# Moving a weight slice to another queue, new planned landing times, and 90 instead of 95 pairs of exponentials on VectorE

## The chip, the cores and the metric

The kernel runs on one core of a Trainium2 chip. The metric is the device time of one execution in microseconds (us). Four runs of the kernel before took 880.51 to 882.28 us, with a median of 881.9. The engines are named as the profile names them: PE (TensorE, with PEld for its weight loads), DVE (VectorE), ACT (ScalarE), POOL (GpSimd) and SP (SyncE, which only issues transfers here). SPq and ACTq in a row are transfers being issued by these engines.

## The reference

Two branches work on the same x (2048 tokens, 640 wide) and are mixed by a gate. Branch A is a short causal convolution of k over four steps, a product with v, a convolution along all 2048 tokens by FFT, and a product with x. Branch B is attention with 32 heads of 20 columns that share one k and one v.

```python
def _B_ref(x, wq, wk, wv, wo):
    q = (x @ wq).reshape(B, S, 32, 20).transpose(0, 2, 1, 3)
    k, v = x @ wk, x @ wv                       # one head of 20 columns
    p = softmax(einsum("bhqd,bkd->bhqk", q, k) * 20 ** -0.5)
    o = einsum("bhqk,bkd->bhqd", p, v)
    return o.transpose(0, 2, 1, 3).reshape(B, S, 640) @ wo

x = A_q
g = sigmoid((x * gate_w).sum(-1, keepdims=True))
a = _A_ref(x, A_k, A_v, A_shift_k, A_ssm_k, A_ssm_D)
b = _B_ref(x, B_wq, B_wk, B_wv, B_wo)
return g * a + (1 - g) * b
```

All inputs and the output are bf16.

## The kernel before

**A planner writes the order.** The kernel first builds a graph of operations (`Op`: an engine, a function that emits the instruction, what it depends on, a price in us, a priority). `Scheduler.run` then plays the five engines against each other with these prices and puts each operation into its engine's list. Only the order of these lists, and the semaphore waits that follow from the dependences, go into the program: prices and latencies in the code are never executed. On the chip each engine works through its list strictly in order, and an instruction that waits holds up all that stand behind it. The planner's numbers are `LAT` (L17, 0.12 us from the end of one operation to the start of one on another engine that depends on it), `SLACK` (L18), the price functions `c_ps`, `c_fast`, `c_exp`, `c_act`, `c_pool`, `c_mm` (L595 to L616), and, for transfers, `nbytes / 300e3` plus `lat` (L432 to L438).

**The attention stream.** Scores are computed in tiles of 128 keys by 512 queries for one head: 4 query blocks x 8 groups of four heads x 16 key blocks x 4 heads = 2048 tiles. `stream` (L1096) walks over 32 groups G and 16 key blocks j. ACT takes the exponential of most tiles, in units that are alternately three tiles wide (written to ETA) and two tiles wide (ETB), one ACTIVATE for each unit (L1161). Their scores come from `QK` (L1136, matmuls at L1129) into PSUM banks 0 to 2 and 3 to 4, and their products with v go through `PV` (L1202) into bank 6. The next unit's scores can be written only when ACT has read the same banks two units earlier. For the j named in `DVE_J[G]` (L590), two of the four tiles, "a pair", go to DVE: `DEXP` (L1165) computes a polynomial exponential in five instructions (two L1191, then L1194, L1195, L1197). Its score matmuls ride along with those of a unit, and its products with v are added before the group's last product. L590 names 95 pairs.

**Side work.** PE, DVE and POOL fit the rest into the stream: the query projections of later blocks (`qproj`, L1047 and L1058), the convolution over four steps (L1385), the FFT as matmuls with cosine and sine tables (`spectra` L1442, `mac` L1475 on POOL, `inverse` L1508) and the output projection (L1538, L1301). On PE such a matmul may be planned ahead of the next score matmuls if its price is not above the planned gap plus `SLACK` (L362, L372). If nothing fits, filler matmuls (L1590) are planned.

**Before the stream.** `loads` (L788) issues four blocks of x on SP, and on ACT's queue the key weights wkr, the value weights wvr, the first slice of the query weights (100 KB, 80 of 640 columns, into `wqst`) and the gate weights gwr. SP issues the rest of the query weights after the last x block has landed. PE transposes x (L960); DVE and ACT copy the transposes to `xT` (L675, L676). While PE has nothing, `pick_work` (L386) plans filler matmuls (L1595). `weights` copies wkr and wvr (L933) and gwr (L935) into one tile on DVE, and the slice of the query weights into `wq_pad` on POOL (L938). Then come the first query group (L1047, L1058), a bound on its length (L1062, L1070, L1076, and a small transfer of the row `cr` into qT), keys, values and gate for each x block in one group of matmuls ("kvn", L987), the squared length of the keys (L995, L1006), its maximum (L1009 to L1023), and the keys with that bound in an added row (L979, L1033, L1031). Beside this run the sine tables: arguments on DVE (L859, L862), the function on ACT (L864). The first exponential needs the first query group with its row, and the first 128 keys, which wait for the maximum over all four blocks.

**After the stream** the last group is normalised and projected (`tail`, L1308).

Of the kernel before, what the change touches and what calls it, by code (L numbers as in the profile page):

```python
# [15 lines left out]
NLANES = 40  # L16
LAT = 0.12  # L17
SLACK = 0.3  # L18
FILL = 0.7
# [18 lines left out]
class Op:  # L38
    __slots__ = ("eng", "fn", "deps", "cost", "kind", "name", "prio", "grp", "alts", "port", "nbytes", "main",
                 "cont", "nun", "succ", "ready", "start", "end", "placed", "sig", "value", "lane", "known", "seq",  # L40
                 "banks", "last", "urge", "floating", "tail", "attached", "lat", "iss", "row", "soft", "cols", "hole")

    def __init__(self, eng, fn, cost, kind, name, prio):
        self.eng = eng
        self.fn = fn
# [112 lines left out]
class Scheduler:  # L158


    def __init__(self, graph, bank_free=(0, 1, 2, 3, 4, 5, 6, 7)):
        self.g = graph
        self.order = {e: [] for e in ENGS}
        self.linear = []
        self.t = {e: 0.0 for e in ENGS}
        self.bank_ready = {b: 0.0 for b in range(8)}
# [103 lines left out]
    def pool_may(self, t):  # L270
# [7 lines left out]
        return bool(w) and t > min(w)  # L278

    def pick_pe(self, t):  # L280
        op = self.pick_work(t)
# [15 lines left out]
        return made[0]  # L297

    def pick_work(self, t):
        q = self.main_q["pe"]  # L300
        p = self.main_pos["pe"]
        m = q[p] if p < len(q) else None
        gap = 1e9
        self.gap = 0.0
        if self.float_left:
# [32 lines left out]
        if m is not None:  # L338
# [5 lines left out]
            if m.nun == 0:  # L344
                r = m.ready
                ok = True
                for b in m.banks or ():
                    if not self.bank_claimed[b]:
                        if self.bank_busy[b]:
                            ok = False  # L350
                        r = max(r, self.bank_ready[b])
                if ok:
                    if r <= t:
                        self.main_pos["pe"] += 1
                        return m
                    gap = r - t
        sw = SWITCH if self.mode != "f" else 0.0
        self.gap = gap if m is not None else 0.0
        if self.open is not None:
            gr = self.open  # L360
            mm = gr.mms[gr.pos]
            if mm.ready <= t and mm.cost + sw <= gap + SLACK and (sw == 0.0 or gap + SLACK - sw >= ROOM):  # L362
                return mm
            return None
        if self.mode != "f" and self.main_started and gap + SLACK - sw < ROOM:
            return None
        best = None
        held = any(gr.rides and gr.ready <= t for gr in self.gcand)
        for gr in self.gcand:
            if gr.rides and t - gr.ready < PATIENCE:  # L370
                continue
            if gr.ready <= t and gr.mms[0].cost + sw <= gap + SLACK:  # L372
                b = None
# [38 lines left out]
    def place(self, op, e):  # L412
# [64 lines left out]
        if gr is not None:  # L477
# [4 lines left out]
            elif op in gr.evacs:  # L482
                if all(x.placed for x in gr.evacs):
                    b = gr.bank
                    self.bank_busy[b] = False
                    self.bank_last[b] = [gr.mms[-1]] + list(gr.evacs)
                    self.bank_ready[b] = max(x.end for x in gr.evacs) + LAT
        for s in op.succ:
            s.nun -= 1
            lat = 0.0 if (s.eng == "pe" and e == "pe") else LAT  # L490
            s.ready = max(s.ready, op.end + lat)
# [103 lines left out]
def c_ps(n):  # L595
    return 0.16 + 1.04e-3 * n
# [6 lines left out]
def c_exp(n):  # L603
    return 0.0633 + 0.8333e-3 * n

# [5 lines left out]
def c_pool(n):  # L611
    return 0.21 + 1.78e-3 * n

# [5 lines left out]
class Kernel:  # L619
# [419 lines left out]
    def qproj(self, I, gs, prio, banks, ng):  # L1039
# [4 lines left out]
        for gl, gi in enumerate(gs):  # L1044
            gr = self.group("qp", prio, banks=banks)
            for dc in range(NDC):
# [4 lines left out]
                if dc == 0:  # L1051

                    o.deps.update(self.crow0 or ())
                    if self.crow0:
# [62 lines left out]
    def attention(self):  # L1117
# [18 lines left out]
        def QK(n):  # L1136
# [10 lines left out]
            for k, (G, j, r) in enumerate(un):  # L1147
# [502 lines left out]
```

## Time and profile before

| | |
|---|---|
| median of four runs | 881.9 us |
| the profiled execution | 881.93 us, of which the span of the profile is 880.1 |
| busy on PE / ACT / DVE / POOL | 856.4 / 855.5 / 717.1 / 377.0 us |
| first exponential starts | 25.27 us |
| last exponential ends | 870.44 us |
| exponentials on ACT | 372 of three tiles, 371 of two |
| pairs on DVE | 95 |

A row of a timeline gives start, length, engine, line, operation, the tile written and the tiles read, and in brackets the idle time before it and what ended that. A row of groups gives the same for all instructions of a line: how often, busy time in all, mean length, idle time before them.

Busy time of each engine in five stretches (columns: stretch, its length, then busy us and number of instructions for PE, PEld, DVE, ACT and POOL, then the clock granted to PE, the transfers' share and GB/s):

```profile
0.00:25.27 25.27, 18.76 (x196) 11.68 (x199) 14.23 (x51) 12.96 (x22) 7.89 (x28) 0.93 0.52 145
140.00:675.00 535.00, 528.44 (x4815) 213.22 (x4811) 458.24 (x550) 532.87 (x471) 264.37 (x223) 1.00 0.08 23
675.00:790.00 115.00, 113.43 (x1120) 45.02 (x1117) 99.25 (x106) 115.00 (x103) 64.04 (x51) 1.00 0.04 12
790.00:870.44 80.44, 79.88 (x683) 34.61 (x679) 44.70 (x65) 80.44 (x71) 3.81 (x3) 1.00 0.25 71
870.44:880.10 9.66, 4.76 (x38) 2.78 (x36) 6.19 (x10) 0.00 (x0) 0.00 (x0) 0.88 0.20 69
```

### The profile page before, as it was taken

The numbers are of one execution on the slowest core, as the hardware profiler recorded it, in microseconds if no ns is written. First come the engines' busy times: TensorE is split into PE (matmuls) and PEld (weight loads), VectorE is DVE, ScalarE is ACT, GpSimd is POOL, SyncE is SP. The second block draws the span as 40 slices with busy tenths as digits, with TensorE's granted clock in tenths as the row PEclk, the third lists the DMA queues.
The fourth block names the chain that finished last, engine by engine and source line by source line (L and its number), as shares of the span: only waits on it lengthen the run. The fifth ranks groups of instructions, "written<-read, shape, count | busy, mean of one in ns | idle before, by whom it ended". The sixth has DMA issues, their size and how long they took to land.

```text
span 880.1 us, 18454 instructions
## 1 busy us (share of the span) xinstructions
PE 856.4 (97%) x7939; PEld 351.3 (40%) x7956; DVE 717.1 (81%) x909; ACT 855.5 (97%) x765; POOL 377.0 (43%) x351
## 2 busy tenths in 40 slices
PE   7999999999999999999999999999999999999997
PEld 4334433334334433344433323444343444324433
DVE  5668998998999888986889898778778888888444
ACT  4999999999999999999999999999999999999995
POOL 2663001445665154564352652344747335760000
PEclk9999999999999999999999999999999999999999
DMA  5910020000100000020000011100010000004221
GB/s 160 216 39 8 20 43 21 19 6 17 43 21 20 15 18 10 19 44 20 13 12 16 21 43 40 31 16 12 19 44 20 14 14 11 5 28 96 66 73 38
DMA packets 49712, 30.69 MB, mean 35 GB/s; under 512 B 32477, under 2 KB 45662, under 8 KB 49630
## 3 DMA queue, kind: packets, MB, share of 16 engines
q1 hardware_dynamic: 48254, 29.03, 12.2%
q8 instruction: 62, 1.02, 0.5%
q10 hardware_dynamic: 1376, 0.48, 0.3%
q14 instruction: 20, 0.16, 0.1%
HBM read 17.85 MB, written 6.02 MB: 27 GB/s over the span
## 4 chain that ended last, share of the span: by engine, by line
ACT 66%; PE 30%; DVE 3%; DMA 1%; issue 0%; ACTq 0%; DVEq 0%
ACT ETA L1161 39%; ACT ETB L1161 26%; PE ps L1129 9%; PE ps L1442 7%; PE ps L1202 5%; PE ps L1508 3%; PE ps L1538 2%; PE ps L1590 1%; DMA gwr<-in_gate_w_dram 1%; PE ps L1301 1%; DVE ETd L1197 1%; DVE dX L1195 1%; PE ps L979 0%; DVE dW L1191 0%; PE ps L1446 0%; DVE dX L1194 0%
## 5 line engine op out<-in xcount | busy, mean ns | idle before, releaser
L1161 ACT ACTIVATE ETA<-ps 128x1536 bf16<-128x1536 f32 x372 | 572.9, 1540 | 3.0 <-PE ps L1129 2.4
L1161 ACT ACTIVATE ETB<-ps 128x1024 bf16<-128x1024 f32 x371 | 415.0, 1119 | 0.5 <-PE ps L1129 0.5
L1129 PE MATMUL ps<-qT,kT 32*128 32x512 bf16 x2048 | 297.8, 384 | 9.6 <-ACT ETA L1161 4.5
L1475 POOL TENSOR_TENSOR Pp<-X,K 128x512 f32<-128x512 bf16 x120 | 158.8, 1340 | 154.3 <-DVE ETd L1197 36.4
L1191 DVE TENSOR_SCALAR dW<-ps 128x512 f32<-128x512 f32 x190 | 130.5, 687 | 63.6 <-PE ps L1129 62.3
L1129 PEld LDWEIGHTS ps<-qT,kT 32*128 32x128 bf16 x2048 | 73.4, 91 | 233.9 <-ACT ETB L1161 110.9
L1202 PE MATMUL ps<-ETA,vaug 128*32 128x512 bf16 x1116 | 153.1, 385 | 0.0
L1202 PE MATMUL ps<-ETB,vaug 128*32 128x512 bf16 x742 | 147.3, 385 | 0.0
L1197 DVE SCALAR_TENSOR_TENSOR ETd<-dX,dW 128x1024 int16<-128x1024 f32 x95 | 134.0, 1411 | 5.5 <-PE ps L1202 5.1
L1195 DVE SCALAR_TENSOR_TENSOR dX<-dX,dW 128x1024 f32<-128x1024 f32 x95 | 136.4, 1436 | 0.3
L1194 DVE SCALAR_TENSOR_TENSOR dX<-dW 128x1024 f32<-128x1024 uint16 x95 | 134.3, 1413 | 0.9
L1475 POOL TENSOR_TENSOR AB<-Pp 128x256 bf16<-128x256 f32 x80 | 65.0, 812 | 88.8 <-DVE dX L1194 32.8
L1442 PE MATMUL ps<-ssm_kT,Tcs 128*128 128x256 bf16 x600 | 95.5, 275 | 0.4 <-DVE dW L1191 0.4
L1442 PE MATMUL ps<-kv,Tcs 128*128 128x256 bf16 x600 | 89.2, 275 | 0.0
L1508 PE MATMUL ps<-AB,Tcs 128*128 128x256 bf16 x600 | 88.8, 274 | 0.0
L1590 PE MATMUL ps<-Tcs,zeros 128*32 128x512 bf16 x980 | 81.0, 385 | 1.1 <-DVE acc L1264 0.6
L1475 POOL TENSOR_TENSOR Pp<-Pp 128x512 f32<-128x512 f32 x40 | 57.3, 1432 | 52.7 <-DVE dX L1194 16.1
L1276 POOL TENSOR_TENSOR oTn<-acc,rbc 128x512 bf16<-128x512 f32 x24 | 41.2, 1717 | 71.1 <-DMA rbc<-scr_d 28.8
L1442 PEld LDWEIGHTS ps<-ssm_kT,Tcs 128*128 128x128 bf16 x600 | 48.3, 97 | 44.3 <-issue 31.4
L1442 PEld LDWEIGHTS ps<-kv,Tcs 128*128 128x128 bf16 x600 | 49.5, 98 | 37.5 <-issue 30.2
L1508 PEld LDWEIGHTS ps<-AB,Tcs 128*128 128x128 bf16 x600 | 51.3, 98 | 31.8 <-issue 26.7
L1202 PEld LDWEIGHTS ps<-ETA,vaug 128*32 128x32 bf16 x1116 | 29.9, 94 | 36.1 <-issue 34.5
(131 smaller groups left out, 634.5 us busy)
## 6 DMA issues: line engine op xcount, KB each, us to landing
rbc<-scr_d SPq DMA_DIRECT2D x31, 256.0 KB
scr_o<-oTn SPq DMA_DIRECT2D x24, 128.0 KB, 1.7
xn<-in_A_q_dram SPq DMA_DIRECT2D x4, 640.0 KB
kv<-in_A_v_dram SPq DMA_DIRECT2D x4, 640.0 KB, 5.0
out_dram<-outsb SPq DMA_DIRECT2D x14, 160.0 KB, 2.4
oTp<-scr_o SPq DMA_DIRECT2D x12, 160.0 KB, 2.5
wog<-in_B_wo_dram SPq DMA_DIRECT2D x4, 200.0 KB
wo<-in_B_wo_dram SPq DMA_DIRECT2D x4, 200.0 KB
```

The lines of the kernel that those rows point to most:

```text
L1129: return e.matmul(self.bank(bk), T["kT4"][32 * r:32 * r + 32, 128 * j:128 * j + 128], T[f"qT{G // 8 % 2}"][32 * r:32 * r + 32, G % 8, :], ...
L1161: op("act", lambda e: e.activation(et(n)[:, 0:w], self.ps[:, lo:lo + w], ACT.Exp, scale=SCALE), [("ps", base[n % 2] + k) for k in range(le ...
L1191: self.evac(gr, "dve", lambda e, bk, h=h: e.tensor_scalar(W[:, 512 * h:512 * h + 512], self.bank(bk), SCALE * LOG2E * 128.0, 128.0 * (127 ...
L1194: V(lambda e: e.scalar_tensor_tensor(X[:, :], w, DP, w, ALU.add, ALU.mult), [kW], ["dX"], c_ps(1024), **k)
L1195: V(lambda e: e.scalar_tensor_tensor(X[:, :], X[:, :], DQ, w, ALU.add, ALU.mult), [kW], ["dX"], c_ps(1024), **k)
L1197: V(lambda e: e.scalar_tensor_tensor(T[f"ETd{pe}"][:, :].bitcast(dt.int16), X[:, :], DA, W[:, :], ALU.mult, ALU.add), [kW, "dX"], [("ETd", ...
L1202: return op("pe", lambda e: e.matmul(self.bank(6)[32 * r:32 * r + 32, :], T[va][:, j, :], src, start=(j == 0), stop=(j == NSC - 1), tile_p ...
L1276: self.pool(lambda e: e.tensor_tensor(out, T["acc"][:, :], T["rbc"][:, :], ALU.mult), ["acc", "rbc"], [key], c_pool(512), prio=p, port=Tru ...
L1442: self.mm(gr, lambda e, bk, lhs=lhs, rhs=rhs, comp=comp, n=n: e.matmul(self.bank(bk, 256, 256 * comp), lhs, rhs, start=(n == 0), stop=(n = ...
L1475: f = lambda e: e.tensor_tensor(out, a, b, alu)
L1508: self.mm(gr, lambda e, bk, lhs=lhs, fc=fc, comp=comp, h=h: e.matmul(self.bank(bk, 256, 256 * h), lhs, AB[:, fc, :, comp, :], start=(fc == ...
L1590: sch.filler = [[lambda e, r=r, st=st: e.matmul(self.bank(6)[32 * r:32 * r + 32, :], self.T["zeros"][:, 0:32], self.T["Tcos"][:, 0, 0:512] ...
```

## The change

Three things change.

First, the load of the slice `wqst[:, :, 0:80]` moves from ACT's queue to SP's, where it stands between x block 0 and x block 1. The gate weights follow directly on the value weights on ACT's queue.

Second, the planner's numbers for the time before the stream: an engine's clock starts at 0.75 instead of 0, the latency from one engine to another comes from a table `LATS` (0 to 0.27) and is 0.03 after a transfer, and each load has a new size and latency. In the stream the latency is `LATX` (0.12) for all, and the slack is 0.3 as before, now under the names SLA, SLB and SLACK0. The price of POOL's operations and of DVE's copy of a query group change a little. `room` is defined and not called.

Third, `DVE_J` is another list, with 90 pairs: 0 0 2 1 3 4 3 3 in the first eight groups (before 0 2 3 2 4 4 2 3), then 4 5 0 4 4 1 3 3 (3 4 4 2 3 1 5 2), 3 4 4 2 2 3 2 4 (4 4 4 1 4 4 1 5) and 4 1 5 2 4 3 3 4 (5 3 1 5 5 2 1 2).

```diff
-LAT = 0.12
-SLACK = 0.3
+LAT = 0.1
+LATS = {("pe", "act"): 0.27, ("act", "pe"): 0.265, ("pe", "dve"): 0.2, ("act", "dve"): 0.265, ("act", "pool"): 0.265,
+        ("dve", "pe"): 0.06, ("dve", "act"): 0.06, ("dve", "dve"): 0.0, ("dve", "pool"): 0.08, ("act", "act"): 0.1,
+        ("pool", "pool"): 0.0}
+BEGIN = 0.75
+LATX = 0.12
+CEX = 0.0633
+LATM = {}
+SLA = 0.3
+SLB = 0.3
+SLACK = 0.05
+SLACK0 = 0.3
...
-        self.t = {e: 0.0 for e in ENGS}
+        self.t = {e: BEGIN for e in ENGS}
...
+    def bank_wait(self, m):
+        return any(self.bank_busy[b] and not self.bank_claimed[b] for b in m.banks or ())
...
+    def lat_of(self, op, a, b):
+        if self.main_started:
+            return LATM.get((a, b), LATX)
+        return 0.03 if op.kind == "d" else LATS.get((a, b), LAT)
+
+    def room(self, m, r):
+
+        q, p = self.main_q["act"], self.main_pos["act"]
+        u = m.unit
+        if p > u:
+            return 0.0
+        return max(self.t["act"] + sum(q[i].cost for i in range(p, u)) - 0.216 - LATS["pe", "act"] - r, 0.0)
...
+                if m.unit is not None and not self.bank_wait(m):
+                    slack = SLB if m.unit % 2 else SLA
+        if slack is None:
+            slack = SLACK0
...
-            if mm.ready <= t and mm.cost + sw <= gap + SLACK and (sw == 0.0 or gap + SLACK - sw >= ROOM):
+            if mm.ready <= t and mm.cost + sw <= gap + slack and (sw == 0.0 or gap + slack - sw >= ROOM):
...
-                    self.bank_ready[b] = max(x.end for x in gr.evacs) + LAT
+                    self.bank_ready[b] = max(x.end + (LATX if self.main_started else LATS[x.eng, "pe"]) for x in gr.evacs)
...
-            lat = 0.0 if (s.eng == "pe" and e == "pe") else LAT
+            lat = 0.0 if (s.eng == "pe" and e == "pe") else self.lat_of(op, e, s.eng)
...
-DVE_J = [(), (3, 11), (1, 6, 11), (2, 11), (2, 6, 10, 14), (3, 4, 9, 12), (3, 9), (1, 6, 11), (2, 8, 13), (1, 2, 7, 12), (2, 6, 10, 14), (3, 9), (1, 7, 10), (8,), (1, 4, 7, 10, 13), (3, 9), (1, 4, 8, 13), (2, 4, 8, 12), (1, 6, 11, 14), (6,), (3, 5, 8, 10), (1, 4, 8, 12), (8,), (1, 4, 7, 10, 13), (1, 4, 7, 10, 13), (1, 6, 11), (4,), (1, 4, 7, 10, 14), (2, 5, 8, 12, 14), (4, 11), (5,), (2, 9)]
+DVE_J = [(), (), (4, 11), (6,), (1, 6, 11), (1, 5, 11, 14), (3, 8, 10), (3, 7, 12), (1, 5, 9, 13), (1, 4, 5, 8, 13), (), (2, 3, 11, 13), (1, 4, 8, 12), (5,), (1, 5, 11), (1, 6, 11), (1, 8, 11), (2, 4, 11, 14), (2, 8, 11, 14), (5, 11), (3, 9), (2, 8, 13), (3, 8), (2, 6, 11, 14), (2, 6, 10, 14), (13,), (1, 4, 7, 10, 13), (2, 7), (1, 7, 9, 13), (1, 5, 12), (1, 6, 11), (2, 4, 10, 14)]
...
-    return 0.0633 + 0.8333e-3 * n
+    return CEX + 0.8333e-3 * n
...
-    return 0.21 + 1.78e-3 * n
+    return 0.3 + 1.68e-3 * n
...
+        wq = aps["B_wq"].rearrange("(p dc) n -> p dc n", dc=NDC)
         for b in range(NB):
-            xl = self.dma(T["xn"][:, 4 * b:4 * b + 4, :], x[:, 4 * b:4 * b + 4, :], writes=[("xn", b)], nbytes=655360,
-                          prio=-9 + b, lat=3.0)
+            xl = self.dma(T["xn"][:, 4 * b:4 * b + 4, :], x[:, 4 * b:4 * b + 4, :], writes=[("xn", b)], nbytes=440000,
+                          prio=-9 + b, lat=5.3)
+            if b == 0:
+                self.dma(T["wqst"][:, :, 0:80], wq[:, :, 0:80], writes=[("wqst", 0)], nbytes=300000, prio=-8.5, lat=5.3)
         self.xl = [xl]
         for n, w, pr in (("wkr", "B_wk", -98.8), ("wvr", "B_wv", -98.7)):
             self.dma(T[n][:, :, :], aps[w].rearrange("(p dc) c -> p dc c", dc=NDC), writes=[n], eng="act",
-                     prio=pr, lat=3.5)
-        wq = aps["B_wq"].rearrange("(p dc) n -> p dc n", dc=NDC)
-        self.dma(T["wqst"][:, :, 0:80], wq[:, :, 0:80], writes=[("wqst", 0)], eng="act", prio=-98.65,
-                 lat=4.5)
+                     prio=pr, lat=4.5)
         self.dma(T["gwr"][:, :], aps["gate_w"].rearrange("(p dc) -> p dc", dc=NDC), writes=["gwr"],
-                 eng="act", prio=-98.6, lat=3.5)
+                 eng="act", prio=-98.6, lat=5.5)
...
-                          qt[:, gi, :], self.bank(bk), T["qup"][:, 0:1], None, ALU.add)), c_ps(512)),
+                          qt[:, gi, :], self.bank(bk), T["qup"][:, 0:1], None, ALU.add)), c_ps(512) + 0.055),
...
+                o.unit = n
```

More of the change, by code (lines that the diff above doesn't have):

```diff
@@ L40 @@
                  "cont", "nun", "succ", "ready", "start", "end", "placed", "sig", "value", "lane", "known", "seq",
-                 "banks", "last", "urge", "floating", "tail", "attached", "lat", "iss", "row", "soft", "cols", "hole")
+                 "banks", "last", "urge", "floating", "tail", "attached", "lat", "iss", "row", "soft", "cols", "hole", "unit")
     def __init__(self, eng, fn, cost, kind, name, prio):
+        self.unit = None
         self.eng = eng
@@ L303, in pick_work @@
         gap = 1e9
+        slack = None
         self.gap = 0.0
@@ L361, in pick_work @@
             mm = gr.mms[gr.pos]
-            if mm.ready <= t and mm.cost + sw <= gap + SLACK and (sw == 0.0 or gap + SLACK - sw >= ROOM):
+            if mm.ready <= t and mm.cost + sw <= gap + slack and (sw == 0.0 or gap + slack - sw >= ROOM):
                 return mm
             return None
-        if self.mode != "f" and self.main_started and gap + SLACK - sw < ROOM:
+        if self.mode != "f" and self.main_started and gap + slack - sw < ROOM:
             return None
@@ L371, in pick_work @@
                 continue
-            if gr.ready <= t and gr.mms[0].cost + sw <= gap + SLACK:
+            if gr.ready <= t and gr.mms[0].cost + sw <= gap + slack:
                 b = None
```

## The prediction

> **What bounds the kernel.** I read the page's busy times first, then the groups by line, the timeline of the first 26 us, the chain of waits there, and at last the ends of the exponentials one by one.
>
> ```profile
> PE 856.4 (97%) x7939; PEld 351.3 (40%) x7956; DVE 717.1 (81%) x909; ACT 855.5 (97%) x765; POOL 377.0 (43%) x351
> L1161 ACT ACTIVATE ETA<-ps 128x1536 bf16<-128x1536 f32 x372 | 572.9, 1540 | 3.0 <-PE ps L1129 2.4
> L1161 ACT ACTIVATE ETB<-ps 128x1024 bf16<-128x1024 f32 x371 | 415.0, 1119 | 0.5 <-PE ps L1129 0.5
> ```
>
> PE and ACT both show 97%, but PE's share holds 980 filler matmuls (L1590) that exist to keep it busy. ACT's is real: it runs exponentials without a break. Their records overlap, so the 1540 and 1119 ns are not prices; from end to end they cost 1.344 us (three tiles) and 0.916 us (two), the median over the stream. The kernel is therefore three pieces: 25.27 us until the first exponential starts, 845.2 us of stream (to 870.44), and 9.66 us of tail. In the stream, 372 x 1.344 + 371 x 0.916 = 839.8 us is work; the first one ends 1.45 us after its start, 0.1 more than its price. Adding every end-to-end distance above the median gives 5.3 us of stalls: 0.57 at the second exponential, about 4.2 in some twenty waits of 0.06 to 0.75 us between 140 and 675 us, nearly none elsewhere. Two of them:
>
> ```profile
> 146.06 1.45 ACT L1161 ACTIVATE ETA<-ps 128x1536 bf16<-128x1536 f32 x1 [0.25 <-PE ps L1129]
> 178.70 1.45 ACT L1161 ACTIVATE ETA<-ps 128x1536 bf16<-128x1536 f32 x1 [0.65 <-PE ps L1129]
> ```
>
> Each time the score matmuls (L1129) stood behind side work in PE's order. So three things can change the time: the start, the number of tiles on ACT, and the stalls. The start, from the timeline and then from the chain of waits:
>
> ```profile
> 2.36 1.18 ACTq L642 DMA_DIRECT2D gwr<-in_gate_w_dram x1
> 7.63 1.28 PE L960 MATMUL ps<-ident,xn 128*128 128x128 bf16 x20
> 11.01 0.52 POOL L938 COPY wq_pad<-wqst 128x400 bf16<-128x400 bf16 x1 [6.03 <-DMA wqst<-in_B_wq_dram]
> 11.46 0.18 DVE L935 COPY wkv<-gwr 128x5 bf16<-128x5 bf16 x1 [4.63 <-DMA gwr<-in_gate_w_dram]
> 12.21 0.94 ACT L864 ACTIVATE Tcs<-tprod,cols 128x770 bf16<-128x770 int32 x1 [2.91 <-DVE tprod L862]
> 13.16 0.87 PE L960 MATMUL ps<-ident,xn 128*128 128x128 bf16 x12 [3.10 <-DVE xT L675]
> 25.27 1.45 ACT L1161 ACTIVATE ETA<-ps 128x1536 bf16<-128x1536 f32 x1 [0.92 <-PE ps L1129]
> ```
> ```profile
> 2.36 9.08 DMA gwr<-in_gate_w_dram
> ```
>
> The gate weights, 1.2 KB, are the last on ScalarE's queue behind the 100 KB slice of the query weights, and land at 11.44. DVE's copy of them (L935) stands in order ahead of everything else on DVE: 4.63 us idle, then ACT waits 2.91 for a table and PE 3.10 for a copy of x. All four x blocks have landed by 12.22 (landing records: 5.99, 8.12, 10.49, 12.22), yet the last one's transposes start only at 19.02.
>
> **The change, part by part.**
>
> *Loads.* The slice moves to SP behind x block 0. SP issues five loads instead of four before its first wait; the added issue (0.62 us, its row on ScalarE) puts the last x issue at about 3.0 us, before block 0 has landed: hidden; with no backlog in the ring it would delay blocks 1 to 3 by those 0.62. Its 640 packets of 15.3 ns over 16 engines are 0.6 us, which blocks 1 and 2 now wait instead of sharing; block 3 still lands near 12.2, as the bytes ahead of it are the same. ScalarE loses a 0.62 us issue ahead of its table load; ACT idles from 6.1 to 8.3 anyway, so nothing. The slice then lands near 7 instead of 10.96 and the gate weights, now directly behind wvr (landed 6.21), between 6.2 and about 8. DVE's 4.63 us wait falls to under 1.5.
>
> A rule against this part: the Trainium skill (DMA: Bandwidth & Descriptors, "Issuing engines are not separate DMA queues") says that loads from different engines share the same 16 DMA engines and that spreading them saves only issue time. By it alone moving the slice would give 0.6 us and the sum would be 884.6. The row above disagrees in this case because what matters is the place in a queue, not which queue: 1.2 KB took 9.08 us.
>
> *Planned landings.* The planner now expects block 0 at 0.75 + 0.1 + 440000/300e3 + 5.3 = 7.62 us (before: 0.1 + 655360/300e3 + 3.0 = 5.28). Until then it puts fillers on PE (L1595) whenever its busy share of the last 2.4 us is under 0.55: about seven at once, then one per 0.36 us at its own price of 0.218. By that count before has 13; the trace shows 12. After it is about 16, four more. They ran at 0.427 us each until 7.45 and cost 0.216 once the clock was up, so block 0's transposes start at 7.63 + 4 x 0.216 = 8.5, at 9.3 if the clock comes late. This gives back 0.9 of the gain.
>
> *From there to the first exponential.* PE's work until the last kvn group ends, at the spacings of rows at full clock: 80 transposes x 0.056 = 4.5, 80 kvn x 0.0253 = 2.0, five query matmuls x 0.216 = 1.1, one L1070 0.2: 7.8 us. The chain behind it (square, sums, maximum, kT, scores) is 25.27 - 21.58 = 3.7 us and stays. 8.5 + 7.8 + 3.7 = 20.0. I add 0.5 for waits that the order leaves: start at **20.5**, a gain of 4.8. Lower end: landing of block 3 plus today's 6.25 us from its transposes to the first exponential, 18.5. Upper end: PE goes slow again as it did after its idle stretch:
>
> ```profile
> 14.28:17.69 3.41, 3.41 (x38) 2.56 (x37) 2.36 (x8) 1.66 (x4) 0.23 (x2) 0.50 0.54 187
> ```
>
> (PE, PEld, DVE, ACT, POOL busy; then PEclk, 0.50.) Against the full-clock spacings this cost 0.85 on query matmuls, 0.2 on kvn, 0.55 on transposes: 1.6. With it and late fillers (0.8) the start is 22.9. DVE and ACT work in the same stretch (10.3 and 10.4 us of 17.9) fits beside PE.
>
> *Pairs.* The list L590 has 90 entries instead of 95 (counted), two tiles each. ACT gets 2048 - 180 = 1868 tiles: 374 units of three and 373 of two, two more of each: 2 x 1.344 + 2 x 0.916 = **+4.5 us**, with nothing to hide it, as ACT is the bound. DVE loses 5 x (2 x 0.687 + 1.413 + 1.436 + 1.411) = 28 us, worth nothing by itself: DVE is 81% busy. By place: groups 0 to 4 (26.4 us each) go from 11 pairs to 6, groups 5 to 24 from 65 to 62, groups 25 to 31 from 19 to 22; the last four from 10 to 14. Those four cost DVE 22.5 us where it idles 35.7 (790 to 870 us: 44.7 busy of 80.4), so they hide; without that idle time the last scores' sums would wait up to 5.6 us for one pair.
>
> *Stalls.* In the stream the planner keeps its numbers: 0.12 for every latency (LATX), 0.3 for every slack (SLA, SLB and SLACK0), and `room`, LATM and CEX change nothing. GpSimd's price moves by 0.04 to 0.06, the qT copy's by 0.055. But a new start and list give a new order, and how many score matmuls come late in it no row shows. Ends: all stalls gone, -5.3; twice as many, +5.3. The nearest row is the stretch from 140 to 675 us, where all but 0.7 lie; it loses 3 of 65 pairs, and the three longest waits there sum to 1.5. I take -1.2, a little under what would go with these three.
>
> *Tail and rest.* 9.66 us, same instructions: 0.
>
> **Sum**, against the profiled execution (881.93; span 880.1 and 1.8 around it; the median is 881.9): 881.93 - 4.8 + 4.5 - 1.2 = **880.4**.
>
> **Rivals.**
>
> 1. *The replay removes the stalls.* For: the waits are short and are the planner's own placements, between 30 and 140 and from 675 us on there are hardly any, and the list was redrawn throughout. Against: the planner's stream prices are the old ones. Stalls of 1.0 in place of 5.3: 881.93 - 4.8 + 4.5 - 4.3 = 877.3.
> 2. *New stalls take the place of the old (slower).* Place: score matmuls behind side matmuls, groups 5 to 24, where PE has the spectra (L1442, L1508) and 62 pairs. The order is a new one there, each such wait costs 0.1 to 0.75, and ACT no longer has five pairs taken off. It decides from stalls above 7.3 us, where the sum passes 883.7; at 10 the time is 881.93 - 4.8 + 4.5 + 4.7 = 886.3. Against: fewer pairs need fewer riding score matmuls.
> 3. *The start barely moves.* More fillers and PE at half clock: start 22.9, 881.93 - 2.4 + 4.5 - 1.2 = 882.8, or 884.0 with today's stalls. For: PE's order is strict and 12 fillers already end 1.4 us after block 0 has landed. Against: PE's long idle stretch came from DVE's wait, which goes.
>
> **Chances.** 880.4 within 878.5 to 883: 0.42 (0.19 of it below 880.1, 0.21 no change, 0.02 slower). Rival 1: 0.26, faster. Rival 2: 0.22, slower. Rival 3: 0.10, half no change, half slower. 0.2% is 1.8 us, about what can be told for this kernel: faster 0.45, same 0.26, slower 0.29. As both signs hold much, the forecast's own range is 878.5 to 883; the range for 8 in 10 goes from 876.3 (rival 1 with one us more of start) to 886.3 (rival 2's price).
>
> **What would show it.** In the changed profile: L935 no longer waits over 1.5 us for gwr; about 16 L1595 rows ahead of the first L960 row, which starts near 8.5; PEclk at 1.00 from then on; the first ETA row near 20.5; x374 and x373 in the two L1161 groups; stalls worked out from their ends near 4. I am wrong if the first ETA row starts before 19 or after 22, if the stalls leave 2 to 7 us, or if the stretch from the last exponential to the end is not 9.7.

## The result, and the profile after

The changed kernel takes **883.03 us** (median of 41 runs, 882.21 to 883.75) against 881.94 for the kernel before (64 runs): a ratio of 1.0015, with a 95% interval of 1.0011 to 1.0019. That is 1.1 us slower, where 1.5 us faster was forecast. The profiled execution took 883.19 us, its span is 881.4.

The page of the changed kernel, busy times and the two groups of exponentials (columns as before):

```profile
PE 859.9 (98%) x7995; PEld 351.9 (40%) x8015; DVE 699.9 (79%) x885; ACT 860.2 (98%) x768; POOL 395.7 (45%) x351
L1194 ACT ACTIVATE ETA<-ps 128x1536 bf16<-128x1536 f32 x374 | 576.8, 1542 | 2.8 <-PE ps L1161 1.3
L1194 ACT ACTIVATE ETB<-ps 128x1024 bf16<-128x1024 f32 x373 | 418.6, 1122 | 1.0 <-PE ps L1161 1.0
```

ACT is the bound as before, with two more units of each size. Its start, from the timeline of the changed kernel:

```profile
1.69 0.45 ACTq L674 DMA_DIRECT2D gwr<-in_gate_w_dram  x1
2.81 5.63 PE L1628 MATMUL ps<-ident,zeros 128*128 128x512 bf16 x15 [2.81 <-DVE ident L852]
6.33 0.60 POOL L970 COPY wq_pad<-wqst 128x400 bf16<-128x400 bf16 x1 [1.04 <-DMA wqst<-in_B_wq_dram]
6.47 0.49 DVE L967 COPY wkv<-gwr 128x5 bf16<-128x5 bf16 x1
8.28 1.28 PE L992 MATMUL ps<-ident,xn 128*128 128x128 bf16 x20
21.01 1.45 ACT L1194 ACTIVATE ETA<-ps 128x1536 bf16<-128x1536 f32 x1 [0.92 <-PE ps L1161]
```

The gate weights landed at 6.05 us instead of 11.44 and the first slice of the query weights at 6.28 instead of 10.96. DVE's copy of the gate weights (L967, before L935) no longer waits for a transfer. Fifteen fillers stand ahead of the first transposes. The stretch that ran at half clock before is gone (a stretch, its length, busy us of PE, PEld, DVE, ACT and POOL, then the granted clock, 1.00, where it was 0.50):

```profile
14.28:17.69 3.41, 3.35 (x86) 3.11 (x86) 2.56 (x12) 2.60 (x7) 0.77 (x4) 1.00 0.65 209
```

So the time can be laid out in the forecast's own terms. Stalls are worked out as there: from the end of one exponential to the end of the next, less 1.344 us for three tiles or 0.916 for two.

| us | before | after | moved | forecast |
|---|---|---|---|---|
| first exponential starts | 25.27 | 21.01 | -4.26 | -4.8 |
| exponentials' own work | 839.8 | 844.3 | +4.5 | +4.5 |
| stall of the second exponential | 0.57 | 1.11 | +0.54 | |
| all later stalls | 4.70 | 5.16 | +0.46 | |
| both stalls together | 5.27 | 6.27 | +1.00 | -1.2 |
| last exponential to the end | 9.69 | 9.63 | -0.06 | 0 |

The moves sum to +1.2, and the spans (880.13 and 881.35) differ by as much. The forecast's sum, 880.4, missed the profiled execution by 2.8 us; 2.2 of them are the stalls, 0.5 the start.

### The profile page after: what moved, and what is told of

Its sections match the earlier page's. It is cut to its first block, busy times and chain, and to the rows that moved or that the text cites. A ratio compares the mean times of both kernels' runs of the same rounds, so it can differ in the third digit from the quotient of the medians.

```text
span 881.4 us, 18539 instructions
## 1 busy us (share of the span) xinstructions
PE 859.9 (98%) x7995; PEld 351.9 (40%) x8015; DVE 699.9 (79%) x885; ACT 860.2 (98%) x768; POOL 395.7 (45%) x351
## 3 DMA queue, kind: packets, MB, share of 16 engines
HBM read 17.85 MB, written 6.02 MB: 27 GB/s over the span
## 4 chain that ended last, share of the span: by engine, by line
ACT 58%; PE 39%; DVE 2%; issue 1%; DVEq 0%; POOL 0%; POOLq 0%
ACT ETA L1194 35%; ACT ETB L1194 23%; PE ps L1161 11%; PE ps L1475 9%; PE ps L1235 7%; PE ps L1541 3%; PE ps L1571 2%; PE ps L1623 2%; PE ps L1079 2%; PE ps L1334 1%; PE ps L1628 1%; PE ps L992 0%; PE ps L1479 0%; PE ps L1102 0%; DVE dW L1224 0%
## 5 line engine op out<-in xcount | busy, mean ns | idle before, releaser
L1508 POOL TENSOR_TENSOR Pp<-X,K 128x512 f32<-128x512 bf16 x120 | 169.7, 1427 | 170.1 <-DVE dX L1228 68.5
L1224 DVE TENSOR_SCALAR dW<-ps 128x512 f32<-128x512 f32 x180 | 123.4, 685 | 62.3 <-PE ps L1161 60.8
L1230 DVE SCALAR_TENSOR_TENSOR ETd<-dX,dW 128x1024 int16<-128x1024 f32 x90 | 128.1, 1423 | 19.7 <-PE ps L1235 19.6
L1227 DVE SCALAR_TENSOR_TENSOR dX<-dW 128x1024 f32<-128x1024 uint16 x90 | 127.1, 1412 | 1.3
L1508 POOL TENSOR_TENSOR AB<-Pp 128x256 bf16<-128x256 f32 x80 | 73.2, 915 | 65.3 <-DVE dX L1227 21.0
L1623 PE MATMUL ps<-Tcs,zeros 128*32 128x512 bf16 x1036 | 85.3, 385 | 0.6 <-DVE acc L1297 0.3
L1508 POOL TENSOR_TENSOR Pp<-Pp 128x512 f32<-128x512 f32 x40 | 54.7, 1369 | 47.8 <-DVE ETd L1230 16.1
L1309 POOL TENSOR_TENSOR oT<-acc,rbc 128x512 bf16<-128x512 f32 x7 | 11.1, 1580 | 77.3 <-DMA rbc<-scr_d 52.1
```

The source lines that it names most:

```text
L1224: self.evac(gr, "dve", lambda e, bk, h=h: e.tensor_scalar(W[:, 512 * h:512 * h + 512], self.bank(bk), SCALE * LOG2E * 128.0, 128.0 * (127 ...
L1227: V(lambda e: e.scalar_tensor_tensor(X[:, :], w, DP, w, ALU.add, ALU.mult), [kW], ["dX"], c_ps(1024), **k)
L1230: V(lambda e: e.scalar_tensor_tensor(T[f"ETd{pe}"][:, :].bitcast(dt.int16), X[:, :], DA, W[:, :], ALU.mult, ALU.add), [kW, "dX"], [("ETd", ...
L1309: self.pool(lambda e: e.tensor_tensor(out, T["acc"][:, :], T["rbc"][:, :], ALU.mult), ["acc", "rbc"], [key], c_pool(512), prio=p, port=Tru ...
L1508: f = lambda e: e.tensor_tensor(out, a, b, alu)
L1623: sch.filler = [[lambda e, r=r, st=st: e.matmul(self.bank(6)[32 * r:32 * r + 32, :], self.T["zeros"][:, 0:32], self.T["Tcos"][:, 0, 0:512] ...
```

## The experiments

Most kernels below are spliced. One planner setting gives each engine's order up to the first exponential, another gives order and PSUM banks from there on.

```python
first, rest = plan(START, True), plan(STREAM, False)    # until the first exponential; all of it
order = {e: [o for o in first[0][e] if o in early] +
            [o for o in rest[0][e] if o not in early and o.name != "fill"] for e in ENGS}
```

"Before's start" and "the change's start" mean the part with loads and prologue, "stream" the rest with its list of pairs. Each kernel was timed against before on the same chip (medians 881.9 to 882.3 there).

### Which part does what: h_start, h_list, h_move, h_back

h_start: the change's start, before's stream with 95 pairs.

> The order until the first exponential is that of the changed kernel (load on SP, 15 fillers, new planned landings); from there on every engine's order, the banks and the 95 pairs are those of the kernel before. Theory 1, the pieces simply add: first exponential near 21.0 us, 743 exponentials, stalls 5.3 to 5.8 us as before (0.6 or 1.1 at the second exponential), tail 9.7, time 881.9 - 4.3 = 877.7 (877.2 to 878.3). Theory 2, the stream's order fits one start only, which is why a new list was needed: the earlier start brings stalls of 8 us or more or a longer tail, time 880.5 or more.

h_list: before's start, the change's stream with 90 pairs.

> The reverse: the order until the first exponential is that of the kernel before (25.3 us), the stream's order and the 90 pairs are those of the changed kernel. Theory 1: 881.9 + 4.5 for ten more tiles + 0.5 for the stalls inside the stream (5.2 against 4.7 us) + 0 to 0.5 at the second exponential = 886.9 to 887.4. Theory 2, the new list is only good with its own start and other things hide part of the ten tiles: 885.5 or less.

h_move: before, with nothing but the slice's load moved to SP's queue behind the first x block.

```diff
+order["act"].remove(wqload)
+order["sp"].insert(1, wqload)
```

> The kernel before, with one instruction moved: the load of the first slice of the query weights is issued by SP behind x block 0 instead of by ACT ahead of the gate weights. Every other order is that of the kernel before, 12 fillers and 95 pairs. Theory A, the load's place alone brings the start forward (PE's order before the stream is the same in both kernels but for three fillers): first exponential at 20.5 to 21.8 us, time 877.5 to 878.6. Theory B, the order by landing times does it: first exponential at 24 us or later, time 880.7 or more.

h_back: h_start with the slice's load back on ACT's queue, ahead of the gate weights.

```diff
+order["sp"].remove(wqload)
+order["act"].insert(order["act"].index(gload), wqload)
```

> The start's order of the changed kernel and the stream of the kernel before, but the load of the slice is back on ACT's queue ahead of the gate weights. Theory A: the slice lands near 11 us and the gate weights near 11.4 again, DVE's copy of the gate weights and POOL's copy of the slice wait 4 us or more, first exponential at 24.5 us or later, time 881.2 or more. Theory B: first exponential near 22 us, time 878.7.

| kernel | time, us | ratio to before (95%) | first exponential | second's stall | later stalls |
|---|---|---|---|---|---|
| h_start | 878.04 | 0.9956 (0.9942 to 0.9969) | 20.82 | 1.11 | 4.71 |
| h_list | 886.96 | 1.0059 (1.0047 to 1.0072) | 25.12 | 0.76 | 5.17 |
| h_move | 877.25 | 0.9948 (0.9936 to 0.9961) | 20.33 | 0.56 | 4.70 |
| h_back | 882.98 | 1.0010 (1.0000 to 1.0020) | 25.16 | 1.11 | 4.73 |

The two halves add up: -4.0 for the start and +5.0 for the new stream make +1.0, and the whole change moved the time by 1.1. The new stream costs the 4.5 us of its tiles and 0.5 of later stalls; whether the list of pairs or the small changes of price placed those stalls was not tried. The 1.11 at the second exponential comes with the change's start: h_start and h_back have it too. The moved load alone takes 4.8 us off, more than the whole new start; the new order of the prologue without the move gives nothing. These two rows of h_back are the waits of before again (POOL's and DVE's copies of the two weights):

```profile
10.78 0.52 POOL L1075 COPY wq_pad<-wqst 128x400 bf16<-128x400 bf16 x1 [4.96 <-DMA wqst<-in_B_wq_dram]
11.24 0.18 DVE L1072 COPY wkv<-gwr 128x5 bf16<-128x5 bf16 x1 [4.38 <-DMA gwr<-in_gate_w_dram]
```

The new order is even 0.5 us later than the old one once the load is moved (20.82 in h_start against 20.33 in h_move, where the granted clock rose to 1.00 at 7.08 and 7.10 us): it holds three more fillers ahead of the first transposes, which start at 8.09 us instead of 7.46. The forecast had put 0.9 us on that. In the changed kernel's own profile, with 21.01, the clock rose a little later, at 7.35 us. h_start and h_list came out as theory 1 had it and h_back as theory A; h_move as theory A too, but with start and time 0.2 us ahead of its ranges.

### Why the moved load helps: h_swap

h_swap: before, with the slice left on ACT's queue and the gate weights issued ahead of it.

```diff
+order["act"].remove(wqload)
+order["act"].insert(order["act"].index(gload) + 1, wqload)
```

> The kernel before with two loads exchanged on ACT's queue: the gate weights ahead of the slice of the query weights; nothing moves to SP. Theory A1, what held the start was the gate weights' place behind the slice: gate weights land near 6.5 us, the slice near 11 as before, x blocks as before; PE transposes x blocks 0 and 1 meanwhile and waits for the slice's copy until about 11.7; first exponential 20.3 to 21.5 us, time 877.2 to 878.5. Theory A2, the slice itself also had to come earlier: PE idles until 11.7 and the clock falls, first exponential at 22 us or later, 879 or more.

878.92 us, ratio 0.9961 (0.9947 to 0.9975), first exponential 21.85, stalls as before. Neither theory's range was met: the start lies between them, and the clock did not fall. In its timeline the gate weights' copy starts at 7.49 us after a wait of 0.99; the slice still comes at 11.19, and the query matmuls (L1187) wait 1.27 us for its copy. The last row is the slice's copy in h_move:

```profile
7.49 0.18 DVE L1075 COPY wkv<-gwr 128x5 bf16<-128x5 bf16 x1 [0.99 <-DMA gwr<-in_gate_w_dram]
11.19 0.66 POOL L1078 COPY wq_pad<-wqst 128x400 bf16<-128x400 bf16 x1 [6.30 <-DMA wqst<-in_B_wq_dram]
11.90 1.25 PE L1187 MATMUL ps<-xT,wq_pad 128*128 128x512 bf16 x5 [1.27 <-POOL wq_pad L1078]
21.85 1.45 ACT L1302 ACTIVATE ETA<-ps 128x1536 bf16<-128x1536 f32 x1 [0.92 <-PE ps L1269]
```
```profile
6.22 0.57 POOL L1075 COPY wq_pad<-wqst 128x400 bf16<-128x400 bf16 x1 [1.72 <-DMA wqst<-in_B_wq_dram]
```

Of the 4.9 us by which h_move's first exponential is earlier, 3.4 come without any load on another queue: 1.2 KB no longer stand behind 640 packets of 160 bytes, and DVE and the clock go free (the granted clock is 1.00 from 7.13 us on, without the slow stretch). The other 1.5 us come from the slice landing about 5 us earlier: the same query matmuls start at 10.39 in h_move. The Trainium skill (DMA: Bandwidth & Descriptors, "Issuing engines are not separate DMA queues") allows only issue time as a gain of spreading loads over engines, whose transfers interleave. For the 3.4 us the measurement sides with it, as the place in one queue did that. For the 1.5 us more than issue time was gained: the same bytes landed at 6.17 on SP's queue and at 11.14 on ACT's. But on SP's queue they also stand ahead of x blocks 1 to 3. There the slice's packets started between 4.09 and 5.46 us (h_move); on ACT's queue they were spread from 6.29 to 10.55 among those of the x blocks (h_swap). No run changes the queue and keeps the place.

### Can the stalls be planned away: h_pull, h_thin, h_thin2

h_pull: h_move, with the score matmuls of 22 late exponentials put ahead of the side and filler matmuls that stood in front of them on PE, past as much PE work as each was late (`i` is the place of the scores in PE's order, `late` that time).

```diff
+while moved < late + 0.06 and pe[j - 1] is side work or filler:
+    j -= 1
+    moved += pe[j].cost
+pe[j:i + n] = pe[i:i + n] + pe[j:i]
```

> The kernel before with the load moved to SP (first exponential 20.3, 877.25 us measured), and in PE's order the score matmuls of the 22 exponentials that waited in its trace are moved ahead of one to thirteen side or filler matmuls that stood directly before them. Theory S, the stalls are nothing but side work that the planner put ahead of the scores: stalls fall from 5.3 to under 1.5 us, time 873.0 to 874.0. Theory R, the scores could not start earlier (bank not yet read by ACT), or the displaced side work makes other scores late: stalls stay above 3.5 us, time 875.5 or more.

877.41 us, ratio 0.9946 (0.9933 to 0.9959), stalls 0.40 and 4.86: no gain, as theory R had it. The waits moved on to the next units, because the displaced matmuls were still to be done there: unit 178's 0.09 us came back at 180, 298's 0.40 as 0.41 at 300, and 134's 0.75 became 0.12 there, 0.56 at 135 and 0.31 at 136.

h_thin and h_thin2 take the side work itself down: the first meant to leave 56 inner matmuls out, the second issues 60 such matmuls in 32 columns by 32 rows, so that the sequence mixer's result loses what they would have added.

```diff
+for o in thin:      # inner matmuls of side groups ahead of the late scores
+    o.fn = lambda e, f=o.fn: f(Narrow(e))   # out[0:32, 0:32], lhs[:, 0:32], rhs 32 columns
```

> h_move with 56 of the side matmuls (inner frequency terms of the sequence mixer's spectra and inverses, neither the first nor the last of their group) left out, each ahead of one of the 21 exponentials from the third on that waited over 0.04 us, as much PE work as each waited and 0.05 us more; the result of the mixer loses those terms. Theory W (the side matmuls in front of the scores on PE make these waits, and scores alone moved in h_pull pushed them on to the next unit because the work stayed): most of the 4.70 us of waits goes, 1.5 or less stays, time 873.5 to 875 against h_move's 877.25. Theory V (the waits come from elsewhere, from a bank that comes free late or from the signals between the engines, and PE only seems busy): waits stay above 3.5 us and the time within 0.8 us of h_move's.

> In h_thin each of the 56 inner matmuls signals other engines and so was issued whole: what ran was h_move's program again (877.39 against 877.25 us, the same waits to 0.01 us). Here 60 inner matmuls of the side groups, chosen in the same way, are issued in 32 columns by 32 rows instead of 256 by 128, so that each keeps its place and its signals and loses most of its PE time (about 0.1 us each, 60 x 0.1 = 6 us in all, by the pace of 8 matmuls in 1.05 us); the mixer's result loses what they would have added. Theory W (side matmuls in front of the scores on PE make the waits of the exponentials): of h_move's 4.70 us of waits behind the second exponential 2 us or less stays, time 874 to 875.5. Theory V (the waits come from banks, signals or another engine): waits above 3.5 us, time within 0.8 us of h_move's 877.3.

h_thin left nothing out: each of these matmuls signals another engine, and my edit spared all that do. It ran h_move's program once more, 877.39 us, ratio 0.9945 (0.9932 to 0.9957), each wait within 0.02 us of h_move's. h_thin2 took 876.34 us, ratio 0.9933 (0.9919 to 0.9946); its later stalls were 3.52 us instead of 4.70. **Both theories miss**: W's 2 us or less was not reached, V's 3.5 only just. Wait by wait it is clearer. The twenty waits aimed at, without the largest, fell from 3.5 to 1.7 us, so narrower side work does shorten them; three new ones of 0.7 us came up. One of these, 0.38 at unit 320, is not the narrowing's work: PE waited 0.36 us for a transfer that landed about 4.8 us after its issue, where it had landed within 4.36 in h_move and h_thin. And the largest, 0.75 us, stayed at 0.73, because fillers make it and no side work does. In h_move's timeline:

```profile
171.98 0.38 PE L1266 MATMUL ps<-qT,kT 32*128 32x512 bf16 x1 [0.65 <-DVE dW L1329]
172.29 1.05 PE L1734 MATMUL ps<-Tcs,zeros 128*32 128x512 bf16 x16
173.27 0.39 PE L1266 MATMUL ps<-qT,kT 32*128 32x512 bf16 x3
173.76 1.45 ACT L1299 ACTIVATE ETA<-ps 128x1536 bf16<-128x1536 f32 x1 [0.64 <-PE ps L1266]
```

PE waits 0.65 us for DVE to empty a bank for one of DVE's own tiles. After that come sixteen fillers which the planner had put into what it took for a gap, 1.05 us, and the scores of the next unit behind them are late.

Sorting the waits over 0.04 us ahead of three-tile units (the second exponential apart) by what stands on PE before the late scores, looking past products with v:

| | behind fillers | behind side matmuls | other | sum, us |
|---|---|---|---|---|
| before | 4 waits, 1.36 | 16, 2.83 | 0 | 4.19 |
| after | 2, 0.28 | 28, 4.25 | 1, 0.44 | 4.97 |
| h_thin2 | 4, 1.04 | 13, 2.00 | 0 | 3.03 |

So the change did cut the long waits behind fillers, and has more in short ones behind side matmuls. That these matmuls make the waits was tried by narrowing them in before's stream only; for the changed kernel's it is read from their place. The one of 0.44 stands behind the scores and products of a DVE pair. One of the short ones, in the timeline of the changed kernel:

```profile
591.09 1.16 PE L1475 MATMUL ps<-ssm_kT,Tcs 128*128 128x256 bf16 x9
591.53 1.02 ACT L1194 ACTIVATE ETB<-ps 128x1024 bf16<-128x1024 f32 x1
592.18 0.39 PE L1161 MATMUL ps<-qT,kT 32*128 32x512 bf16 x3
592.67 1.45 ACT L1194 ACTIVATE ETA<-ps 128x1536 bf16<-128x1536 f32 x1
```

Nine side matmuls fill PE until the scores at 592.18. The exponential ends at 594.12 and the one ahead of it at 592.55: 1.57 us instead of 1.344, a wait of 0.23 that a list of idle times does not show, since the records overlap.

### Does the planner's allowance set these waits: a_low, a_high

The planner lets a side matmul run over the free gap by `SLA` ahead of a three-tile unit, by `SLB` ahead of a two-tile unit. Both kernels are the changed one with these two numbers changed, 0.3 and 0.3 as they are, and the whole order placed anew.

```diff
-SLA = 0.3
-SLB = 0.3
+SLA = 0.2    # a_high: 0.35
+SLB = 0.1    # a_high: 0.1
```

> The changed kernel with a smaller allowance: SLA, how far a side matmul may run over the free gap ahead of a three-tile unit's scores, 0.2 instead of 0.3 us, SLB (two-tile units) 0.1 instead of 0.3. The order behind the start is placed anew by it; the planner's own tail stays at 10.5 us. Theory A (the waits are side matmuls that the allowance lets in): the waits ahead of three-tile units fall from 4.97 us (31 over 0.04 us, all but two below 0.26 us) by about 0.1 each, to 2 to 3.5 us, time 881 to 882. Theory B (the planner lays the gaps themselves wrongly, so that the allowance doesn't decide): 4.4 us or more, time within 0.7 us of 883.03. First exponential 21.0 and exponentials 747 in both.

> The changed kernel with SLA 0.35 and SLB 0.1 (tail by the planner 10.5 us again), to go with a_low: between the two only SLA differs. Theory A: waits ahead of three-tile units 5 to 6.5 us, at least 2 us more than in a_low, time at least 1.5 us above a_low's. Theory B: within 0.7 us of a_low in both.

a_low: 882.38 us, ratio 1.0009 (0.9999 to 1.0018), 28 waits of 4.37 us. a_high: 882.36 us, ratio 1.0003 (0.9994 to 1.0012), 24 waits of 4.07 us. **Theory A falls**: the larger allowance gave fewer waits, not more, and the times agree; a_low's 4.37 is just under the 4.4 that theory B asked for. The size of a wait hardly depends on it, with a median of 0.15 us in all three. For its own order of the changed kernel the planner foretells 1.2 us of stalls in all, for before's 1.1, where 6.3 and 5.3 were measured; a list of 20 to 30 windows each taken for some 0.15 us longer than they are would fit, but which of its prices is at fault, if any, was not tried and stays open.

### The second exponential: h_indg

h_indg: the changed kernel with the five small DVE instructions at L909 to L914, which build an index matrix, behind the kT copies instead of among them.

```diff
+ind = [o for o in dve if o.seq in range(360, 365)]    # L909, L911, L914
+for o in ind: dve.remove(o)
+dve[last_kT_copy + 1:last_kT_copy + 1] = ind
```

> The changed kernel with one edit: the five small DVE instructions that make the query-side index matrix (lines 909 to 914) stand behind the kT copies instead of between them. In the changed kernel the first of these copies takes 1.70 us beside a POOL memset of 1.97 us, the two kT copies there take 1.63 instead of 1.28 us, and PE then waits 0.37 us for them. Theory I (that is what made the second exponential's wait grow from 0.57 to 1.11 us): its wait falls to 0.4 to 0.7 us, first exponential within 0.2 us of 21.01, time 882.3 to 882.8 against 883.03. Theory M (the memset holds DVE's copies whatever stands among them): the wait stays at 1.0 us or more and the copies at 1.6 us.

882.75 us, ratio 1.0006 (0.9996 to 1.0015); the second exponential's stall went back to **0.56 us**, as theory I had it, while the first exponential started at 21.10. The time is 0.3 us under 883.03, which is the stall's 0.55 less 0.09 of later start and 0.18 of later stalls in its profile, but hardly more than the runs can tell apart. The changed kernel's timeline first, then h_indg's:

```profile
19.75 1.97 POOL L977 MEMSET wq_pad<- 128x2240 int32 x1
20.05 1.70 DVE L914 CAST IndG<-acol 128x4 bf16<-128x4 f32 x1
20.12 1.63 DVE L1063 TENSOR_SCALAR kT<-ps,cols 128x512 bf16<-128x512 f32 x2
21.83 1.25 PE L1011 MATMUL ps<-xT,wk 128*128 128x512 bf16 x5 [0.37 <-DVE kT L1063]
23.47 1.02 ACT L1194 ACTIVATE ETB<-ps 128x1024 bf16<-128x1024 f32 x1 [1.00 <-PE ps L1161]
```
```profile
19.84 1.97 POOL L1085 MEMSET wq_pad<- 128x2240 int32 x1
20.07 1.27 DVE L1171 TENSOR_SCALAR kT<-ps,cols 128x512 bf16<-128x512 f32 x2 [0.29 <-PE ps L1119]
23.00 1.02 ACT L1302 ACTIVATE ETB<-ps 128x1024 bf16<-128x1024 f32 x1 [0.46 <-PE ps L1269]
```

Both have the same memset. With the cast of four columns beside it, the two kT copies take 1.63 us instead of 1.27 and PE waits for a bank. The cast ends at 21.75, 0.03 us after the memset, and so do both copies.

### Can the start be earlier still: h_fill9, h_true, h_true2

h_fill9 (first two lines of the diff): h_move with 9 instead of 12 fillers ahead of the first transposes. h_true: the start planned anew with landing times as traced in h_move, fillers priced at 0.3 us, and before's stream. h_true2: the same, with that price for the start alone.

```diff
+for o in order["pe"][:3]:
+    order["pe"].remove(o)
...
-f = Op("pe", self.filler0, c_mm(512), "c", "fill", 0.0)
+f = Op("pe", self.filler0, FILLC or c_mm(512), "c", "fill", 0.0)   # FILLC 0.3
```

> The kernel before with the load moved to SP, and three of the twelve filler matmuls that stand ahead of the first transposes left out. Theory F, as in the prediction, the fillers hold back x block 0, which has landed by 5.5: transposes start 1.2 us earlier (6.3) and the first exponential comes 0.4 to 1.2 us earlier (19.1 to 19.9), 876.0 to 876.9. Theory G, PE then waits for x block 1 (8.8) anyway, and the transposes of block 0 run at half clock: first exponential within 0.3 of 20.3, 877.0 to 877.5.

> The start is planned again with the landings that the trace of the moved load shows (x at 5.6, 9.0, 10.9, 12.6, slice 6.4), seven fillers ahead of the first transposes and the query group ahead of x block 1; from the first exponential on the order of the kernel before. Theory P, the order before the stream still leaves PE waiting: first exponential at 19.0 to 19.8 us, time 876.0 to 876.8. Theory Q, the chain through PE's work and the last x block is already tight, as the changed kernel's new order won nothing either: first exponential 20.1 to 21.0, 877.0 to 878.0.

> The earlier re-planned start (h_true) had a fault of the splice: the planner's price of a filler was changed for the whole plan, so the order behind the first exponential was placed anew too and was not before's. Here that price holds for the start alone; from the first exponential on, order and banks are before's. Theory P (only the start differs): first exponential about 19.6 us as in h_true, 0.8 earlier than h_move's 20.33, second exponential's wait 1.2 as there (+0.65 against h_move), the other waits near h_move's 4.70, tail 9.7; time 876.5 to 877.5. Theory Q (an earlier start by reordering upsets the stream of before as well): the other waits over 6 us or the tail over 11 us, time over 879, as part of h_true's 890.99 would then come from the start itself.

| kernel | time, us | ratio to before (95%) | first exponential | second's stall | later stalls | to the end |
|---|---|---|---|---|---|---|
| h_fill9 | 877.20 | 0.9938 (0.9919 to 0.9958) | 19.85 | 0.56 | 5.55 | 9.75 |
| h_true | 890.99 | 1.0107 (1.0087 to 1.0127) | 19.55 | 1.21 | 9.94 | 17.55 |
| h_true2 | 877.46 | 0.9946 (0.9934 to 0.9959) | 20.02 | 1.29 | 4.73 | 9.73 |

None beats h_move clear of noise. In h_true the price, meant for the start, had also placed the whole stream anew: a change of 0.08 us in the price of an instruction that does no work cost 8 us in the tail and 5 in stalls. h_true2 confirms it: with before's stream kept, these are gone. Its first exponential came at 20.02, not at the 19.6 expected, though its order up to there is h_true's; what it gains on h_move, 0.3 us, is more than lost at the second. h_fill9's first exponential came as theory F had it, but its time is h_move's, as theory G had it. Its later stalls were 0.85 us longer in its profile, 0.51 of it a new wait at unit 320, where PE waited 0.50 us for the same transfer as in h_thin2. The earlier start is not what made it late: h_thin started at 19.80 and did not wait there.

## Why the prediction was wrong

- **The load's move: right in kind.** The forecast's 4.8 after 0.9 given back means 5.7 for the move alone; h_move's first exponential is 4.9 earlier. Both landings were slightly ahead of the forecast (6.28 against "near 7", 6.05 against 6.2 to 8). DVE's wait of 4.63 went, and the waits of 2.91 on ACT and 3.10 on PE shrank to 0.93 and 0.54. h_swap shows that the place in the queue is most of it. That the other 1.5 us hang on where the slice lands, the forecast had not seen. It also took x block 3 to land near 12.2 as before; it landed at 12.84, and blocks 1 and 2 at 9.37 and 11.13 instead of 8.12 and 10.49. This cost nothing, as PE came to each of them later.
- **Fillers and chain.** 15 fillers (forecast 16), transposes at 8.28 (8.5). From there to the first exponential 11.5 us were summed from spacings and 0.5 allowed for waits; it took 12.73, and 12.87 in h_move. The allowance was too small: PE waited 0.54 for a copy of x at 10.10 alone, and one filler at 16.53 took 0.22. The 0.73 too little, less the 0.22 by which the transposes came early, are the 0.5 us by which the start fell short.
- **Pairs: right.** +4.5 us, on ACT's own price, with nothing hiding it; h_list shows it with 0.5 us of stalls on top. DVE's lighter load (699.9 instead of 717.1 us busy) bought nothing.
- **Stalls: the failed step.** It said "I take -1.2, a little under what would go with these three" (the three longest waits). Long ones did go: of four waits over 0.35 us one is left, of 0.44, and those behind fillers shrank from 1.36 to 0.28 us. But the term had no place for new ones, although its own text says that no row shows them: 1.4 us more stand behind side matmuls, 0.44 behind a DVE pair, and 0.54 came at the second exponential, where a reordered small cast met a memset. So the stalls moved by +1.0 and not by -1.2. Rival 2 named the mechanism and set it at more than 2 us of growth; it was 1.0. With both ends open to the same degree, 0 was the fair middle, and the sum would have been 881.6, still 1.6 us under the profiled execution.
- **Tail and clock: right**, 9.63 and 1.00 once it was up.

The version that beats both is h_move: 877.25 us, the list of 95 pairs, the old order, one load moved.

## What to carry to other kernels

Split a change with several parts before taking it whole: here one moved transfer was worth 4.8 us, and the stream with its new list, built for a new planner setting, gave 5.0 back. Where an engine is the bound, work handed back to it costs its full price, and an order planned anew is a new draw of short waits that shows in no old profile. A small transfer that a whole engine waits for goes first in its queue; ask what stands ahead of it there, and what the other queues send beside it.

## What the runs showed of the hardware

- **The clock's rise is a matter of chance within about two microseconds, and the start with it.** h_move and h_thin are one program: the granted clock rose at 7.10 and 6.02 us, the first exponential started at 20.33 and 19.80, all later waits agree to 0.02 us. h_thin2, with the same order up to there, has 8.20 and 20.92, which makes about 0.5 us of start for each us by which the clock rises later. The change's start has the same slope, from 6.76 and 20.67 in a_low to 7.87 and 21.22 in a_high. It does not hold for every order: h_true and h_true2 share theirs and had 8.63 and 19.55, 6.15 and 20.02. So differences of half a microsecond at the start, h_fill9's 0.48 (its clock rose at 8.71) among them, are not told from chance by one profile. The Trainium skill (TensorE: Matmul & The Clock Gate, "What's actually happening") says that the window is free-running and the number of cold matmuls differs from run to run; these two profiles agree.
- **A mostly busy PE can lose its clock, and the busy share alone does not tell when.** In h_true's stream the clock went to half for 3.41 us after 3.42 us in which PE was busy for 2.27 (66%) and its longest wait was 0.99, near the end. After another such stretch of the same profile, with 2.25 us busy and no wait over 0.93, it stayed at 1.00. What told the two apart stays open (windows; columns as above):

```profile
745.90:749.32 3.42, 2.27 (x22) 0.71 (x19) 3.39 (x4) 3.42 (x4) 1.58 (x1) 1.00 0.00 0
749.32:752.73 3.41, 3.41 (x28) 0.71 (x27) 3.41 (x4) 1.22 (x2) 1.75 (x2) 0.50 0.02 5
790.28:793.70 3.42, 2.25 (x28) 0.56 (x24) 3.39 (x6) 2.32 (x3) 3.42 (x3) 1.00 0.00 0
793.70:797.11 3.41, 3.31 (x43) 0.96 (x43) 3.41 (x4) 3.41 (x5) 2.08 (x2) 1.00 0.02 2
```

- **A tiny DVE instruction is not always tiny.** The cast of four columns took 1.70 us beside POOL's memset, in the changed kernel and in h_start, and ended 0.03 us after it both times. The next two casts of the changed kernel took 0.17 and 0.16. The wider kT copies beside the same memset took 0.75 and 0.61 us in h_indg, so not every DVE instruction is held.
